# Two weight loads shared between SyncE and GpSimd, and a new order for the opening of an attention-and-experts kernel

## The chip, the cores and the metric

One core of a Trainium2 chip runs the whole program. The metric is device time in microseconds (us): the median of three runs of the kernel before is 735.4 us (737.32, 734.79, 735.40).

## What is computed

Three layers follow one another, all in float32 precision:

```python
f = 1 / (1 + exp(-f_logit))                                # [4, 8, 768, 48]
for t in range(768):                                       # decayed linear attention, per batch and head
    state = f[:, :, t, :, None] * state + einsum('bhd,bhe->bhde', k[:, :, t], v[:, :, t])
    y[:, :, t] = einsum('bhd,bhde->bhe', q[:, :, t], state)
x = y.transpose(0, 2, 1, 3).reshape(3072, 384)
h = x @ w_in                                               # [384, 2048]
x = (h - tanh(h)) @ w_out                                  # [2048, 384]
keep = x @ w_skip > 0                                      # rows that are not kept pass through
e, g = argmax(x @ w_gate), softmax weight of that argmax   # 8 experts, one per row
x[keep] += g * (relu(x @ w1[e]) @ w2[e])                   # [384, 1024], [1024, 384]
```

`w_in` and `w_out` arrive as 8-byte floats. The kernel loads them as pairs of 32-bit words and decodes them on the chip.

## The kernel before

The 3072 rows are cut into 24 units of 128 rows (time chunk c, batch b: unit u = 4c + b). Two units make a block of 256 rows.

**Attention, per unit.** SyncE (SP in the profile) issues the loads of f, k, q and v (`load_f` L288, `load_in` L301), 192 KB each. ScalarE and VectorE form log f. PE multiplies it by a triangle (`pl`, L418). From that come scaled k and q (L433, L436), which PE transposes (`pk`, `pq`, L446). `scores` (L467, L487) multiplies them, VectorE masks the result (L496), and `values` (L508, L515, L521) brings in v. `scores` of a unit waits for `values` of the unit before it, because the two share PSUM buffers. When both units of a block are done, the output is copied out. Small copies inside SBUF, called tails (L549), then move some rows to their place: three of them are issued by GpSimd (POOL) and three by ScalarE in the first blocks. `xhi` and `xlo` (L580, L584) split the block into a high and a low part, `xT`.

**Dense layer.** `gemm1` (L651, "G" below) is nine matmuls for each 128 columns of `w_in`, and `gemm2` (L691, "H") is six for each 128 rows of `w_out`; each float32 product is made of three products of high and low parts. G of block 0 needs `xT` of block 0 and the first decoded columns of `w_in`.

**Weights.** `w_in` comes in four loads w0 to w3 (`load_win`), each of twelve DMAs: six of 192 KB and six small ones of 64 KB, which fill 16 partitions each. `w_out` comes in four loads u0 to u3 (`load_wout`), one DMA of 1536 KB each. Every load goes to one of two staging buffers, so w1 waits until the second half of w0 has been read (step `stt2` of chunk 1). It is decoded in two chunks: ScalarE (`abs`, L190), three VectorE operations (L192, L194, L198), then a split in high and low parts (L368, L372).

**The order.** The first 10 of 12 blocks are written as steps. Each step has an engine, a cost, the steps that it comes after, and a key. `in_order` (L35) simulates them and always takes the step that can begin first; among equals, the one with the smallest key. The order that comes out is the order of instructions on every engine, and each engine then runs its list strictly in that order. Costs and keys are not instructions: they only move other instructions. The lines that set the opening's keys are these:

```python
CHUNK0, CHUNK, LATE = -65, 6, 4
QUEUE = (0, 1, "w", 2, 3, "w", "w", "u", "u", "u", 4, 5, "w", "u")
```

Place i of `QUEUE` gives the key 4i - 200 to f of that unit or to that weight load; k and q of the unit follow with +1 and +2, and v with +8. The loads of units 6 and later wait for the weight load with number `LATE` (4 is w1, 6 is u1). The order on SP before is: f, k, q of unit 0; f, k, q of unit 1; w0; v of units 0 and 1; f, k, q of units 2 and 3; v of 2 and 3; u0; units 4 and 5; w1; u1; units 6 to 9. POOL's list in the opening is `initial` (memsets, ending with L785), the decay of the state of each unit (L569), constants, and the tails.

Of the kernel before, what the change touches and what calls it, by code (L numbers as in the profile page):

```python
# [93 lines left out]
def decay_attention_moe_kernel(  # L94
# [14 lines left out]
    nc = tc.nc  # L109
    P = 128  # L110
    B, H, T, D = q.shape
# [17 lines left out]
    FIRST, NJOIN, NPAY, SKEW = 6, 4, 6, 0  # L129
    EARLIEST, LEAD = -100, 32  # L130
    ALONE = 4
    CHUNK0, CHUNK, LATE = -65, 6, 4
    QUEUE = (0, 1, "w", 2, 3, "w", "w", "u", "u", "u", 4, 5, "w", "u")
    LAG = 2

    cpool = ctx.enter_context(tc.tile_pool(name="cpool", bufs=1, side="left"))
# [49 lines left out]
    def bare(stg, c, mark):  # L186

        u, v = stg[..., 1], stg[..., 0]
        ci = c.bitcast(I32)
        nc.scalar.activation(c, u.bitcast(F32), AF.Abs, scale=2.0**-111, accum_out=mark)  # L190
        yield
        nc.vector.tensor_scalar(ci, ci, 3, None, op0=ALU.logical_shift_left)  # L192
        yield
        nc.vector.scalar_tensor_tensor(  # L194
            out=ci, in0=u, scalar=-0x80000000, in1=ci, op0=ALU.bitwise_and, op1=ALU.bitwise_or
        )
        yield
        nc.vector.scalar_tensor_tensor(  # L198
            out=ci, in0=v, scalar=29, in1=ci, op0=ALU.logical_shift_right, op1=ALU.bitwise_or
        )  # L200
        yield

    def fetch(pool, name, shape, pieces, dst, eng):

        n = pieces[0][3]
        if n == 2 or dst is None:
            t = pool.tile(shape + [2], I32, tag="stg", name=f"stg{name}")
        if n == 2:
            to = t.rearrange("p a w c -> p a (w c)")
        else:  # L210
            to = t = t.bitcast(F32)[..., 0] if dst is None else dst
        for rows, a, src, _ in pieces:
            if len(src.shape) == 3:
                eng.dma_start(to[rows, a], src)
            else:
                for i in range(src.shape[1]):
                    eng.dma_start(to[rows, a.start + i].rearrange("p (w c) -> p w c", w=src.shape[2]), src[:, i])
        return t

    def load(pool, name, shape, pieces, dst):  # L220
# [5 lines left out]
    def words(w):  # L226
        return (w.bitcast(I32), 2) if w.dtype != F32 else (w, 1)
# [48 lines left out]
    more = [rest[:, i * H * 64 : (i + 1) * H * 64].rearrange("p (h d) -> p h d", h=H) for i in range(5)]  # L276
# [6 lines left out]
    NFB = 4  # L283

    def load_f(u):
        c, b = divmod(u, B)
        fx[u] = apool.tile([P, H * D], F32, tag="f", name=f"f{u}", bufs=NFB)
        nc.sync.dma_start(  # L288
            fx[u].rearrange("t (h d) -> t h d", h=H), f_logit[b, :, c * P : (c + 1) * P, :].rearrange("h t d -> t h d")
        )  # L290
# [13 lines left out]
    def exp_f(u):  # L304
        nc.scalar.activation(fx[u], fx[u], AF.Exp, scale=-1.0)
# [10 lines left out]
        nc.scalar.activation(hi, raw, AF.Copy)  # L316
        eng.tensor_tensor(lo, raw, hi.bitcast(F32), ALU.subtract)  # L317

    NWC = 8
    NWL = 4  # L320
    stage = {}

    def load_win(j):

        w = DFF // NWL
        src, m = words(w_in)
        rows = src.rearrange("(h r) (w n c) -> n h r w c", r=D, w=NWL, n=NWL)[j]
        pieces = []
        for jj, (h0, h2, h3) in enumerate(((0, 5, 7), (4, 1, 3))):
            o = 64 * jj  # L330
            pieces.append((slice(o, o + D), slice(0, 2), rows[h0 : h0 + 3 : 2].rearrange("h r w c -> r h w c"), m))
            pieces.append((slice(o, o + D), slice(2, 3), rows[h2 : h2 + 1].rearrange("h r w c -> r h w c"), m))
            pieces.append((slice(o + D, o + 64), slice(0, 3), rows[h3].rearrange("(i r) w c -> r i w c", r=16), m))
        stage["w", j] = fetch(spool, f"w{j}", [P, KT, w], pieces, None, nc.sync)

    def load_wout(j):
# [8 lines left out]
    def unpack(a, j):  # L345

        r = NWC // NWL
        raw = stage[a, j // r]
        if a == "w":
            w = DFF // NWC  # L350
            fs, ss = slice(j * w, (j + 1) * w), slice(j % r * w, (j % r + 1) * w)
            hi, lo = whi[:, :, fs], wlo[:, :, fs]
            raw = raw[:, :, ss]
        else:
            n = NF // NWC
            fs, ss = slice(j * n, (j + 1) * n), slice(j % r * n, (j % r + 1) * n)
            hi, lo = uhi[:, fs], None
            raw = raw[:, ss]
        unit = 1.0
        if (w_in if a == "w" else w_out).dtype != F32:  # L360
            stg, raw = raw, spool.tile([P] + list(hi.shape[1:]), F32, tag="dc", name=f"dc{a}{j}")
            n = 2 * j + (a == "u")
            yield from bare(stg, raw, marks[:, n : n + 1])
            unit = 2.0**-8
        else:
            for _ in range(4):
                yield
        nc.scalar.activation(hi, raw, AF.Copy, scale=unit)  # L368
        yield
        if lo is None:  # L370
            lo = ulo[:, fs]
        nc.vector.scalar_tensor_tensor(  # L372
            out=lo, in0=raw, scalar=unit, in1=hi.bitcast(F32), op0=ALU.mult, op1=ALU.subtract
        )
        yield
# [9 lines left out]
    def step(name, key, eng, cost, emit, *after, take=(), give=(), moved=0.0, lag=0.15):  # L385

        made[name] = x = Step(key, eng, cost, emit, after, take, give, moved, lag)
        steps.append(x)
# [564 lines left out]
    def pieces(gen):  # L953

        return lambda: next(gen, None)

    NCHK = 2 * NWC
    chunks = [(a, j + i) for j in range(0, NWC, 2) for a in "wu" for i in range(2)]

# [13 lines left out]
    line, seen_of = {}, {"w": 0, "u": 0}  # L973
    for i, x in enumerate(QUEUE):
        if x in seen_of:
# [4 lines left out]
    for n, (a, j) in enumerate(chunks):  # L980
        at = CHUNK0 + CHUNK * n
        if n % 2 == 0:
            step(
                ("ld", n), line["wu"[n // 2 % 2], n // 4], "SP", 5.4 if a == "w" else 0.45, (lambda a=a, j=j: (load_win if a == "w" else load_wout)(j // 2)),
                ("stt2", n - 3), moved=5.5 if a == "w" else 4.5,
            )
        more = pieces(unpack(a, j))
        step(("abs", n), at, "ACT", 0.9, more, ("ld", n - n % 2), ("lo", n - 2))
        step(("shift", n), at, "DVE", 0.56, more, ("abs", n))
        step(("stt1", n), at, "DVE", 0.95, more, ("shift", n))  # L990
        step(("stt2", n), at, "DVE", 0.95, more, ("stt1", n))
        step(("hi", n), at, "ACT", 0.84, more, ("stt2", n))
        step(("lo", n), at, "DVE", 0.95, more, ("hi", n), ("ulo", 0) if a == "u" else None)
        made["lo" + a, j] = made["lo", n]


    for u in range(NU):
        blk, half = divmod(u, 2)
        e = EARLIEST + 6 * u if u < FIRST else NF * blk - LEAD + 6 * half - 8

        def get(nm, u=u):
            return lambda: load_in(nm, u)

        if u >= FIRST and (u - FIRST) % NFB == 0:
            us = range(u, min(u + NFB, NU))
            for w in us:
                step(("f", w), e - 20, "SP", 0.45, (lambda w=w: load_f(w)), ("pl", w - NFB), ("ld", LATE), moved=1.2)
            for w in us:
                step(("exp", w), e, "ACT", 0.51, (lambda w=w: exp_f(w)), ("f", w))
                step(("min", w), e, "DVE", 0.36, (lambda w=w: min_f(w)), ("exp", w))  # L1010
            step(("lns", u), e, "ACT", 2.6 + 0.5 * len(us), (lambda us=us: ln_f(us)), *[("min", w) for w in us])
            for w in us:
                made["ln", w] = made["lns", u]
        elif u < FIRST:
            step(("f", u), line[u], "SP", 0.45, (lambda u=u: load_f(u)), ("pl", u - NFB), moved=1.2)
            step(("exp", u), e, "ACT", 0.51, (lambda u=u: exp_f(u)), ("f", u))
            step(("min", u), e, "DVE", 0.36, (lambda u=u: min_f(u)), ("exp", u))
            step(("ln", u), e, "ACT", 0.5, (lambda u=u: ln_f([u])), ("min", u))
        w = -1 if u < 4 else u - 4 if u < 6 else u - 2
        hold = ("ld", LATE) if u >= FIRST else None  # L1020
        step(("k", u), line.get(u, e - 19) + 1, "SP", 0.45, get("k"), ("mk", w), hold, moved=1.2)
        step(("q", u), line.get(u, e - 19) + 2, "SP", 0.45, get("q"), ("mq", w), hold, moved=1.2)
        step(("v", u), line.get(u, e - 18) + 8, "SP", 0.45, get("v"), ("values", w), hold, moved=1.2)
        attend(u)


# [5 lines left out]
    for n, (b, f) in enumerate(slots):  # L1032
# [12 lines left out]
        if n < len(slots) - LAG:  # L1045
            p = homes.get(b, "po")
# [5 lines left out]
            if f == NF - 1:  # L1052
                for u in (2 * b, 2 * b + 1):
# [5 lines left out]
                    r = pieces(route(u))  # L1059
                    at = n + LAG + 2 + 7 * (u % 2 if b > 1 else u)  # L1060
# [167 lines left out]
    for g in range(NF2, E * NF2 + LAG):  # L1228
        e, f = divmod(g, NF2)
# [260 lines left out]
```

## Time and profile before

| what | us |
|---|---|
| median of three runs | 735.4 |
| the profiled execution | 737.04 |
| its span in the trace | 734.9 |
| PE busy in the span | 696.7 (95%) |
| VectorE / ScalarE / POOL busy | 491.9 / 367.0 / 283.2 |

The span is what the trace covers; the 2.1 us between it and the execution's time lie around it. PE is the engine of the matrix products. DVE is VectorE, ACT is ScalarE, SP is SyncE, which only issues DMAs; a letter q behind a name is the engine's DMA or instruction queue.

### The profile page before, as it was taken

Reading aid. Unit: us, or ns where it says so; the run is one execution under the profiler, and the core shown is the slowest. Engines: PE = TensorE matmul, PEld = TensorE weight load, DVE = VectorE, ACT = ScalarE, POOL = GpSimd, SP = SyncE. Lnnn points to the kernel's source line nnn. Section 1 sums busy time; section 2 is a strip of 40 time slices with the busy share of each in tenths; the row PEclk is TensorE's granted clock in tenths of the full one; section 3 lists DMA queues with packets and bytes.
Section 4 is the critical chain, followed back from the end, with each engine's and each line's share of the span. In section 5 each row is a group of like instructions: output and inputs, shape, how many; then the busy total and the mean of one; then the engine's idle time right before and its main releaser. Section 6 shows DMA issues by size and latency. Waiting matters only on the chain. (4 is left out here: it accounts for less than half of the span.)

```text
span 734.9 us, 16491 instructions
## 1 busy us (share of the span) xinstructions
PE 696.7 (95%) x6168; PEld 655.8 (89%) x6168; DVE 491.9 (67%) x1390; ACT 367.0 (50%) x882; POOL 283.2 (39%) x316
## 2 busy tenths in 40 slices
PE   5889989999999999999999999999989899999993
PEld 3678989999998999999999999999989689999993
DVE  2678999678777968768685775845583845655530
ACT  3576786446444465456545444444434435555530
POOL 1232443423344343442434343434543314555641
PEclk9999999999999999999999999999999999999997
DMA  9979793833321312222221220033002667666500
GB/s 155 234 136 220 160 158 80 310 64 72 76 39 40 80 37 70 44 61 44 63 61 28 60 42 32 2 97 115 13 28 71 205 202 236 213 207 211 175 14 22
DMA packets 152688, 76.77 MB, mean 104 GB/s; under 512 B 113864, under 2 KB 149337, under 8 KB 152470
## 3 DMA queue, kind: packets, MB, share of 16 engines
q1 hardware_dynamic: 149462, 70.48, 38.6%
q0 software_dynamic: 2848, 5.00, 1.9%
q8 instruction: 50, 0.82, 0.5%
q14 instruction: 40, 0.33, 0.2%
q10 hardware_dynamic: 288, 0.15, 0.1%
HBM read 61.60 MB, written 15.86 MB: 105 GB/s over the span
## 5 line engine op out<-in xcount | busy, mean ns | idle before, releaser
L674 POOL TENSOR_TENSOR gs<-th,gs 128x256 fp32r<-128x256 f32 x190 | 168.1, 889 | 249.5 <-ACT gs L668 225.0
L691 PE MATMUL po<-uhi,gs 128*128 128x384 f32 x768 | 230.6, 343 | 2.0 <-POOL gs L674 1.8
L651 PE MATMUL ph<-xT,whi 128*128 128x256 f32 x1152 | 219.9, 287 | 2.7 <-DVE th L663 1.8
L651 PEld LDWEIGHTS ph<-xT,whi 128*128 128x128 f32 x1152 | 183.9, 189 | 8.0 <-DVE th L663 3.6
L651 PE MATMUL ph<-xT,wlo 128*128 128x256 f32 x576 | 162.6, 282 | 0.0
L691 PEld LDWEIGHTS po<-uhi,gs 128*128 128x128 f32 x768 | 142.4, 190 | 6.4 <-POOL gs L674 3.8
L663 DVE TENSOR_TENSOR th<-ph,th 128x256 f32<-128x256 f32 x192 | 79.9, 419 | 90.8 <-ACT th L658 90.1
L233 DVE CUSTOM_DVE_ANT_0 scr<-pay,wb 128x384 f32<-128x384 f32 x198 | 128.0, 647 | 7.9 <-ACT pay L699 4.1
L691 PE MATMUL po<-ulo,gs 128*128 128x384 f32 x384 | 129.8, 338 | 0.4 <-DVE ulo L372 0.4
L658 ACT ACTIVATE th<-ph 128x256 f32<-128x256 f32 x192 | 72.7, 381 | 113.2 <-PE ph L651 75.9
L668 ACT ACTIVATE gs<-th 128x256 fp32r<-128x256 f32 x192 | 79.2, 416 | 96.4 <-DVE th L663 92.7
L651 PEld LDWEIGHTS ph<-xT,wlo 128*128 128x128 f32 x576 | 109.5, 190 | 0.0
L691 PEld LDWEIGHTS po<-ulo,gs 128*128 128x128 f32 x384 | 73.2, 191 | 0.7 <-DVE ulo L372 0.7
L1150 PE MATMUL eh<-xt,w 128*128 128x256 f32 x504 | 69.6, 283 | 0.0
L1174 PE MATMUL eo<-w,h 128*128 128x384 f32 x336 | 69.1, 342 | 0.0
L1150 PEld LDWEIGHTS eh<-xt,w 128*128 128x128 f32 x504 | 67.0, 188 | 0.4
L1174 PEld LDWEIGHTS eo<-w,h 128*128 128x128 f32 x336 | 56.3, 188 | 0.0
L1159 DVE SCALAR_TENSOR_TENSOR h<-eh,h 128x256 fp32r<-128x256 f32 x56 | 23.7, 423 | 45.5 <-ACT h L1158 45.5
L1158 ACT ACTIVATE h<-eh 128x256 fp32r<-128x256 f32 x56 | 21.5, 385 | 61.9 <-PE eh L1150 61.8
L732 POOL DMA_INDIRECT xs<-pay,di x24 | 25.7, 1069 | 65.5 <-DVE sm L245 31.2
L317 POOL TENSOR_TENSOR w<-r,w 128x768 fp32r<-128x768 f32 x24 | 44.1, 1846 | 12.3 <-ACT w L316 12.2
L891 POOL DMA_INDIRECT out_dram<-yo,xa x16 | 15.7, 979 | 69.3 <-DVE yo L899 33.6
(189 smaller groups left out, 927.8 us busy)
## 6 DMA issues: line engine op xcount, KB each, us to landing
r<-in_moe_w_dram SPq DMA_DIRECT2D x56, 384.0 KB, 5.1
stgu<-in_moe_w_out_dram SPq DMA_DIRECT2D x4, 1536.0 KB, 7.0
f<-in_f_logit_dram SPq DMA_DIRECT2D x24, 192.0 KB, 3.5
stgw<-in_moe_w_in_dram SPq DMA_DIRECT2D x24, 192.0 KB, 5.5
out_dram<-pay SPq DMA_DIRECT2D x24, 192.0 KB, 2.9
k<-in_k_dram SPq DMA_DIRECT2D x22, 192.0 KB, 3.3
q<-in_q_dram SPq DMA_DIRECT2D x22, 192.0 KB, 3.3
v<-in_v_dram SPq DMA_DIRECT2D x22, 192.0 KB, 2.8
```

The costliest lines, as they stand in the source:

```text
L233: nc.vector.tensor_tensor_reduce(out=scr, in0=x, in1=wb[:, n], scale=1.0, scalar=0.0, op0=ALU.mult, op1=ALU.add, accum_out=lg[:, n : n + 1])
L317: eng.tensor_tensor(lo, raw, hi.bitcast(F32), ALU.subtract)
L651: nc.tensor.matmul(ph, lhsT=w[:, i, fs], rhs=x[:, i, a], start=(n == 0), stop=(n == 3 * KT - 1))
L658: nc.scalar.activation(th, ph, AF.Tanh)
L663: nc.vector.tensor_tensor(th, ph, th, ALU.subtract)
L668: nc.scalar.activation(t[:, 0], th, AF.Copy)
L674: eng.tensor_tensor(t[:, 1], th, t[:, 0].bitcast(F32), ALU.subtract)
L691: nc.tensor.matmul(po[blk, s], lhsT=t[:, a, ss], rhs=w[:, f], start=(f == 0 and n == 0), stop=(f == NF - 1 and n == 2))
L732: nc.gpsimd.indirect_dma_start(xs[:, :], bass.IndirectOffsetOnAxis(ap=di[:, :], axis=0), pt[:, :], None, bounds_check=E * NT - 1, oob_is_e ...
L1150: nc.tensor.matmul(ph, lhsT=a1[:, w, i, f * P : (f + 1) * P], rhs=xt[:, i, a], start=(n == 0), stop=(n == 3 * KT - 1))
L1159: nc.vector.scalar_tensor_tensor(out=h[:, 1], in0=ph, scalar=0.0, in1=h[:, 0].bitcast(F32), op0=ALU.max, op1=ALU.subtract)
L1174: nc.tensor.matmul(eo[e, s], lhsT=h[:, a, ss], rhs=a2[:, w, f], start=(f == 0 and n == 0), stop=(f == NF2 - 1 and n == 2))
```

## The change

The six small DMAs of w0 and of w1 are issued by `nc.gpsimd`, that is by POOL; those of w2 and w3 stay on SP. A step ("by", n) without instructions of its own stands for POOL's time in the plan. The costs of the DMA issues in the plan are other ones, `QUEUE` has another order, v has the key +15 in place of +8, and `CHUNK0` and `LATE` are changed.

```diff
+    VAT = 15
-    CHUNK0, CHUNK, LATE = -65, 6, 4
-    QUEUE = (0, 1, "w", 2, 3, "w", "w", "u", "u", "u", 4, 5, "w", "u")
+    CHUNK0, CHUNK, LATE = -60, 6, 6
+    QUEUE = (0, 1, "w", 2, 3, "w", "w", "u", 4, 5, "w", "u", "u", "u")
...
-        for rows, a, src, _ in pieces:
+        for rows, a, src, _, *other in pieces:
+            by = other[0] if other else eng
             if len(src.shape) == 3:
-                eng.dma_start(to[rows, a], src)
+                by.dma_start(to[rows, a], src)
...
-    NWC = 8
+    NWC, NPOOL = 8, 2
...
-            pieces.append((slice(o + D, o + 64), slice(0, 3), rows[h3].rearrange("(i r) w c -> r i w c", r=16), m))
+            pieces.append((slice(o + D, o + 64), slice(0, 3), rows[h3].rearrange("(i r) w c -> r i w c", r=16), m, nc.gpsimd if j < NPOOL else nc.sync))
...
-                ("ld", n), ..., "SP", 5.4 if a == "w" else 0.45, ...
+                ("ld", n), ..., "SP", (3.9 if j // 2 < NPOOL else 7.6) if a == "w" else 0.7, ...
+        if a == "w" and j % 2 == 0 and j // 2 < NPOOL:
+            step(("by", n), line["w", n // 4], "POOL", 5.0, lambda: None, ("stt2", n - 3), ("init", 0), lag=2.0)
-        step(("abs", n), at, "ACT", 0.9, more, ("ld", n - n % 2), ("lo", n - 2))
+        step(("abs", n), at, "ACT", 1.1, more, ("ld", n - n % 2), ("by", n - n % 2) if j // 2 < NPOOL and a == "w" else None, ("lo", n - 2))
...
-            step(("f", u), line[u], "SP", 0.45, ...
+            step(("f", u), line[u], "SP", 0.8, ...
-        step(("v", u), line.get(u, e - 18) + 8, "SP", 0.45, get("v"), ("values", w), hold, moved=1.2)
+        step(("v", u), line.get(u, e - 18) + VAT, "SP", 0.8, get("v"), ("values", w), hold, moved=1.2)
```

The steps of k and q change their cost from 0.45 to 0.8 in the same way.

## Rows read from the trace of the kernel before

**Rows 1.** Page: PE's busy time (share, instructions); DMA's busy tenths in 40 slices

```profile
PE 696.7 (95%) x6168; PEld 655.8 (89%) x6168; DVE 491.9 (67%) x1390; ACT 367.0 (50%) x882; POOL 283.2 (39%) x316
DMA  9979793833321312222221220033002667666500
```

**Rows 2.** Windows by stage, PE alone: stretch, PE busy, clock, DMA share, GB/s

```profile
10.00:15.00 5.00, 4.32 (x36) 1.00 1.16 145
15.00:20.00 5.00, 2.29 (x9) 1.00 1.30 153
...
62.00:91.00 29.00, 28.92 (x307) 1.00 0.85 178
```

**Rows 3.** PE's waits, 0 to 110 us: total us, times, longest

```profile
PE pl L421 <- DVE lfs L409: 1.7, 1, 1.7
...
PE pq L446 <- ACT uhi L368: 1.4, 1, 1.4
...
PE ph L651 <- DVE xT L584: 0.6, 1, 0.6
PE po L691 <- DVE ulo L372: 0.4, 1, 0.4
PE ph L651 <- ACT xT L580: 0.3, 1, 0.3
```

**Rows 4.** SP's timeline: start, us, issue, count

```profile
5.31 8.37 SPq L217 DMA_DIRECT2D stgw<-in_moe_w_in_dram  x12
13.72 1.21 SPq L301 DMA_DIRECT2D v<-in_v_dram  x2
15.24 3.44 SPq L288 DMA_DIRECT2D f<-in_f_logit_dram  x1
...
21.50 0.85 SPq L301 DMA_DIRECT2D early<-in_k_dram  x1
22.39 2.28 SPq L301 DMA_DIRECT2D early<-in_q_dram  x1
...
41.16 13.93 SPq L217 DMA_DIRECT2D stgw<-in_moe_w_in_dram  x12
```

**Rows 5.** SP's timeline, 6.0 to 6.7 us and 12 to 13.7 us alone

```profile
5.31 1.42 SPq L217 DMA_DIRECT2D stgw<-in_moe_w_in_dram  x2
...
12.47 1.21 SPq L217 DMA_DIRECT2D stgw<-in_moe_w_in_dram  x2
```

**Rows 6.** PE's timeline: start, us, operation, count, [idle before <- releaser]

```profile
20.21 1.95 PE L508 MATMUL py<-A,v 128*48 128x128 f32 x16 [1.65 <-DMA v<-in_v_dram]
...
31.06 0.59 PE L521 MATMUL pu<-ident,en 128*64 128x1 f32 x16
31.59 0.65 PE L446 MATMUL pk<-ident,early 128*112 128x128 f32 x4
...
34.20 0.55 PE L467 MATMUL ps<-qT,kT 48*64 48x128 f32 x8 [0.88 <-ACT qT L453]
```

**Rows 7.** Windows of the lull, all engines: PE, PEld, DVE, ACT, POOL busy, clock, DMA

```profile
56.00:58.00 2.00, 1.49 (x10) 1.20 (x11) 2.00 (x4) 2.00 (x5) 0.00 (x0) 0.95 0.66 127
58.00:60.00 2.00, 2.00 (x13) 1.56 (x17) 1.81 (x3) 1.62 (x4) 0.00 (x0) 0.50 1.00 389
60.00:62.00 2.00, 2.00 (x49) 1.83 (x42) 0.30 (x2) 0.00 (x0) 0.00 (x0) 0.70 1.06 366
```

**Rows 8.** POOL's timeline

```profile
24.39 0.68 POOL L569 TENSOR_TENSOR S<-S,dd 112x192 f32<-112x192 f32 x1 [20.23 <-DVE S L559]
...
33.39 1.74 POOL L549 DMA_DIRECT2D early<-early  x3
41.26 0.68 POOL L569 TENSOR_TENSOR S<-S,dd 112x192 f32<-112x192 f32 x1 [6.13 <-DVE S L559]
...
52.10 1.50 POOL L549 DMA_DIRECT2D xf<-tm  x3
```

**Rows 9.** Page, costliest groups: the dearest DMA issue on POOL

```profile
L732 POOL DMA_INDIRECT xs<-pay,di x24 | 25.7, 1069 | 65.5 <-DVE sm L245 31.2
```

More of the change, by code (lines that the diff above doesn't have):

```diff
@@ L211, in fetch @@
             to = t = t.bitcast(F32)[..., 0] if dst is None else dst
-        for rows, a, src, _ in pieces:
+        for rows, a, src, _, *other in pieces:
+            by = other[0] if other else eng
             if len(src.shape) == 3:
-                eng.dma_start(to[rows, a], src)
+                by.dma_start(to[rows, a], src)
             else:
                 for i in range(src.shape[1]):
-                    eng.dma_start(to[rows, a.start + i].rearrange("p (w c) -> p w c", w=src.shape[2]), src[:, i])
+                    by.dma_start(to[rows, a.start + i].rearrange("p (w c) -> p w c", w=src.shape[2]), src[:, i])
         return t
@@ L983, in decay_attention_moe_kernel @@
             step(
-                ("ld", n), line["wu"[n // 2 % 2], n // 4], "SP", 5.4 if a == "w" else 0.45, (lambda a=a, j=j: (load_win if a == "w" else load_wout)(j // 2)),
+                ("ld", n), line["wu"[n // 2 % 2], n // 4], "SP", (3.9 if j // 2 < NPOOL else 7.6) if a == "w" else 0.7, (lambda a=a, j=j: (load_win if a == "w" else load_wout)(j // 2)),
                 ("stt2", n - 3), moved=5.5 if a == "w" else 4.5,
             )
+        if a == "w" and j % 2 == 0 and j // 2 < NPOOL:
+            step(("by", n), line["w", n // 4], "POOL", 5.0, lambda: None, ("stt2", n - 3), ("init", 0), lag=2.0)
         more = pieces(unpack(a, j))
-        step(("abs", n), at, "ACT", 0.9, more, ("ld", n - n % 2), ("lo", n - 2))
+        step(("abs", n), at, "ACT", 1.1, more, ("ld", n - n % 2), ("by", n - n % 2) if j // 2 < NPOOL and a == "w" else None, ("lo", n - 2))
         step(("shift", n), at, "DVE", 0.56, more, ("abs", n))
@@ L1014, in decay_attention_moe_kernel @@
         elif u < FIRST:
-            step(("f", u), line[u], "SP", 0.45, (lambda u=u: load_f(u)), ("pl", u - NFB), moved=1.2)
+            step(("f", u), line[u], "SP", 0.8, (lambda u=u: load_f(u)), ("pl", u - NFB), moved=1.2)
             step(("exp", u), e, "ACT", 0.51, (lambda u=u: exp_f(u)), ("f", u))
@@ L1020, in decay_attention_moe_kernel @@
         hold = ("ld", LATE) if u >= FIRST else None
-        step(("k", u), line.get(u, e - 19) + 1, "SP", 0.45, get("k"), ("mk", w), hold, moved=1.2)
-        step(("q", u), line.get(u, e - 19) + 2, "SP", 0.45, get("q"), ("mq", w), hold, moved=1.2)
-        step(("v", u), line.get(u, e - 18) + 8, "SP", 0.45, get("v"), ("values", w), hold, moved=1.2)
+        step(("k", u), line.get(u, e - 19) + 1, "SP", 0.8, get("k"), ("mk", w), hold, moved=1.2)
+        step(("q", u), line.get(u, e - 19) + 2, "SP", 0.8, get("q"), ("mq", w), hold, moved=1.2)
+        step(("v", u), line.get(u, e - 18) + VAT, "SP", 0.8, get("v"), ("values", w), hold, moved=1.2)
         attend(u)
```

## The prediction

> **What bounds the kernel now.** I read the page first: PE is busy for 696.7 of 734.9 us, and the slices show the DMA engines near full in the first tenth of the span and idle in most of the rest [rows 1]. So the kernel is bound by PE as soon as PE has work, and what an edit of the opening can win is PE's idle or slowed time there. I then read PE alone by stage. From 62 to 91 us it is busy for 28.92 of 29 us: no order can win there. In 15 to 20 us it is busy for 2.29 of 5, while DMA stands at a share of 1.30 and moves only 153 GB/s; a share over 1 means that packets queue at the engines [rows 2]. The third view is PE's waits up to 110 us: 0.6 and 0.3 us at the first G, 1.4 and 0.4 us in a lull near 56 us, and 1.7 us for log f of units 6 and later at 91 us [rows 3]; before them its timeline has 1.65 us for v of unit 0 [rows 6]. Last, the windows of the lull: behind it PE's granted clock falls to 0.50, its lower level of 1.2 GHz, in 58 to 60 us, and is a mean of 0.70 in the next two and 0.95 in the two before [rows 7]. That costs 2 x 0.5 + 2 x 0.3 + 2 x 0.05 = 1.7 us of full-speed work.
>
> **The change, part by part.**
>
> *The six small issues of w0 leave SP.* Two small issues take 1.21 us, two large ones 1.42, and all twelve 8.37 [rows 4, 5]. SP's share becomes 6 x 0.71 = 4.3 us, so SP ends w0 at 9.6 us and not at 13.7. POOL waits 20.23 us before its work at 24.39, thus from 4.2 us on [rows 8], and issues its six there. The trace shows no such issue on POOL. From below, a 16 KB tail takes 1.50 / 3 = 0.5 us [rows 8]; from above, an indirect one takes 1.07 us [rows 9]. That is 3.0 to 6.4 us, all in POOL's gap: no cost. Bytes stay the same.
>
> *v moves behind f, k, q of unit 2.* By key, SP's list is now w0, f2, k2, q2, v0, f3, k3, q3, v1. Three loads at 0.85 us put v0's issue near 12.2 us, 1.5 us before the 13.72 of the trace [rows 4]. But 3 x 192 KB (0.59 MB) more stand in front of it, and at the 153 GB/s of that stretch [rows 2] they take 3.9 us. If SP bound, v0 would come 1.5 us earlier; if the DMA engines do, up to 3.9 us later. The share of 1.30 and SP's issue of f2, which was held for 3.44 us [rows 4], speak for the engines. I take 3.9 - 1.5 = +2.4 us, for `values` of unit 0 at 20.21 us [rows 6] and for all that hangs on it.
>
> The Trainium skill, on the page "DMA: Bandwidth & Descriptors", section "Issuing engines are not separate DMA queues", says that issues from several engines end on the same 16 engines and save only the sequencer's time. By that rule moving the six brings nothing here, since the queue behind SP is full; this is the second rival below. The share over 1 agrees.
>
> *Unit 2 is ready early.* Before, its transposes began at 31.59 us, after `values` of unit 1 had ended at 31.06 + 0.59 = 31.65, and its scores followed at 34.20, with a wait of 0.88 us in between [rows 6]: 2.55 us on the path. A q of that stretch was issued with a stall until 24.67 us [rows 4]; now that of unit 2 is issued near 12 us, and the transposes fit into waits for the mask of unit 1. Two groups of 0.65 us and the wait make 2.2 us; the rest of the 2.55 is log f of unit 3 on PE, which stays. I take -2.0 us (bounds 0 and -2.55).
>
> *First G.* Its two waits, 0.3 and 0.6 us [rows 3], come from the tails of block 0. With unit 3 loaded sooner, the scores of unit 3 can fill them: -0.9 us (bounds 0 and -0.9).
>
> *The lull at 54 to 62 us.* PE waits 1.4 + 0.4 + 0.3 us there; the 0.3 is a wait for a scaled k, too short to have a row here. G of block 1 waits for `xT` of block 1, that is for unit 3, which is ready earlier by what is won above. DVE and ACT, however, are busy for all of 56 to 58 us [rows 7], so the lull is partly theirs and need not go. I take half, -1.0 us (bounds 0 and -2.1), and half of the clock's loss, -0.8 us (bounds 0 and -1.7).
>
> *w1.* SP gave it from 41.16 to 55.09 us, twelve issues for 13.93 us against 8.37 for w0 [rows 4], so it will be in its buffer several us sooner. This hides fully: what needs it lies in the stretch where PE is busy for 28.92 of 29 us [rows 2]. On POOL its six issues wait for the staging buffer, and whatever stands behind them in POOL's list waits too. In the gap between the tails of block 0 (ended by 35.1 us) and the decay at 41.26 us [rows 8] they cost nothing, 3.0 to 6.4 us in a gap of 6.13. I take 0; the bad place is the third rival.
>
> *The rest.* The hold of units 6 and later on u1 changes nothing, as they already stood behind u1. `CHUNK0`, v of later units and the plan's costs only reorder work beneath a full PE: 0, with bounds of 1.7 us on either side for the wait at 91 us, which a new order can lose or double [rows 3].
>
> *The sum:* +2.4 - 2.0 - 0.9 - 1.0 - 0.8 = -2.3 us. The profiled execution took 737.04 us, a span of 734.9 and 2.1 around it, so it would take 734.7. It stands 1.6 us above the median of the runs; against the median the forecast is 735.4 - 2.3 = 733.1 us.
>
> **The rivals.**
>
> *Larger gain.* The small pieces land by a queue of their own and v0 is bound by SP: -1.5 us instead of +2.4. The lull and its clock dip then go wholly: -1.5 - 2.55 - 0.9 - 2.1 - 1.7 = -8.8 us at most. For it: every term has its row. Against it: full DMA engines, and full DVE and ACT in the lull. I expect -4.5 to -8.8: 726.6 to 730.9 us, 728.5 as its middle.
>
> *No change.* The DMA engines set the opening. v0 comes +3.9 us later, unit 2 gives back 2.0 and the first G 0.9, and the lull stays as it is: +1.0, thus 736.4 us, with 734.3 to 737.4 around it. For it speak the shares of 1.16 and 1.30 from 10 to 20 us [rows 2].
>
> *Slower: POOL's tails behind w1.* If POOL's list has the six pieces of w1 before the tails of block 0 (33.39 us [rows 8]), and the buffer comes free only shortly before, the tails start 3.0 to 6.4 us late, and `xT` of block 0 and the first G with them. PE can cover about 2.1 us with the scores of unit 3, so 0.9 to 4.3 us remain. With +2.4 for v0 and -2.0 for unit 2, and nothing won in the lull, that is +1.3 to +4.7 us: 736.7 to 740.1, with 738.4 as its middle. It decides from the moment at which the output of unit 1 is ready before POOL has issued the last piece. For it: w1 is now planned earlier, and the buffer was freed only near 33 us before. Against it: the plan counts 5 us of POOL for it and knows the tails.
>
> The Trainium skill, "SBUF — State Buffer", section "A bandwidth-pool intuition that's wrong (but worth ruling out)", gives a DMA issued by GpSimd 620 ns alone and about 3100 ns beside a VectorE copy that holds the shared port. By its figure the six would take 18.6 us, an estimate, and this rival would cost over 10 us. The tails on POOL in this trace took 0.50 to 0.58 us each beside a busy VectorE [rows 8], so I give that size little weight.
>
> **How the numbers follow.** The forecast (-0.5 to -4.5 us, 730.9 to 734.9) has 0.40, the larger gain 0.17, no change 0.18, slower 0.25. What a measurement can tell from no change is 0.3%, or 2.2 us. Of the forecast's 0.40, 0.25 lies beyond -2.2 us, so faster is 0.25 + 0.17 = 0.42. Of the slower rival's 0.25, 0.03 lies within 2.2 us, so slower is 0.22, and the same is 0.15 + 0.18 + 0.03 = 0.36. The range runs from 728.8 to 738.4: it leaves out the lower half of the larger gain (0.08) and the upper half of the slower rival (0.12).
>
> **What would show it.** Right: in the new trace the wait for v of unit 0 still exists, with v landing at 21 to 24 us; scores of unit 2 follow `values` of unit 1 without transposes in between; the first G waits under 0.3 us; the granted clock after 54 us stays near 1. Wrong: the first G later than 42 us behind POOL's pieces of w1; the DMA share well below 1 before 25 us; a new wait of PE over 2 us anywhere in 62 to 110 us, which would make the prediction fail whatever the opening wins.

## The result, and the profile after

The changed kernel takes 744.03 us (median of 4 runs, 742.4 to 745.15) against 736.36 us for the kernel before (4 runs on the same chip, 734.79 to 738.49): a ratio of 1.0105, with an interval of 1.0077 to 1.0134. It is slower by 7.7 us. The forecast was 733.1 us, and the time lies outside its range of 728.8 to 738.4. The profiled execution took 743.65 us (span 741.7).

The page shows PE with nearly the same busy time as before, 694.6 against 696.7 us [rows 1], in a span that is 6.8 us longer. The extra time is therefore idle time of PE, not more work.

```profile
PE 694.6 (94%) x6168; PEld 656.4 (89%) x6168; DVE 489.7 (66%) x1390; ACT 367.3 (50%) x882; POOL 294.4 (40%) x328
```

PE's waits of the first 115 us (total, times, longest) begin with one that the kernel before does not have [rows 3]:

```profile
PE pg L808 <- DMA wg<-in_moe_w_skip_dram: 6.6, 1, 6.6
PE pl L420 <- ACT f L314: 5.1, 1, 5.1
PE py L510 <- DMA v<-in_v_dram: 3.8, 1, 3.8
```

`pg` is the turn of the router's gate weights: three transposes of `wg`, which stand in this order just ahead of the first G. PE's timeline of after (start, us, operation, count, [idle before <- releaser]), which answers to [rows 6]:

```profile
22.34 1.95 PE L510 MATMUL py<-A,v 128*48 128x128 f32 x16 [3.84 <-DMA v<-in_v_dram]
...
34.91 0.60 PE L523 MATMUL pu<-ident,en 128*64 128x1 f32 x16
35.44 0.65 PE L448 MATMUL pk<-ident,early 128*112 128x128 f32 x4
35.92 0.60 PE L448 MATMUL pq<-ident,early 128*112 128x128 f32 x4
36.45 0.45 PE L469 MATMUL ps<-qT,kT 48*64 48x128 f32 x8
...
47.18 0.60 PE L523 MATMUL pu<-ident,en 128*64 128x1 f32 x16
54.37 0.80 PE L808 MATMUL pg<-ident,wg 128*9 128x128 f32 x3 [6.60 <-DMA wg<-in_moe_w_skip_dram]
54.83 0.78 PE L653 MATMUL ph<-xT,whi 128*128 128x256 f32 x2
```

From 47.78 to 54.37 us PE does nothing, and the first G, ready behind it in PE's list, starts at 54.83. Why `wg` was late stands in SP's timeline of after (start, us, issue, count), beside which [rows 4] can be laid:

```profile
5.50 4.30 SPq L219 DMA_DIRECT2D stgw<-in_moe_w_in_dram  x6
...
12.33 6.02 SPq L303 DMA_DIRECT2D early<-in_q_dram  x1
18.40 0.77 SPq L303 DMA_DIRECT2D v<-in_v_dram  x1
...
41.59 3.81 SPq L219 DMA_DIRECT2D stgw<-in_moe_w_in_dram  x6
45.50 0.71 SPq L303 DMA_DIRECT2D v<-in_v_dram  x1
46.25 0.58 SPq L801 DMA_DIRECT2D wg<-in_moe_w_gate_dram  x1
46.88 2.14 SPq L802 DMA_DIRECT2D wg<-in_moe_w_skip_dram  x1
...
144.45 5.56 SPq L706 DMA_DIRECT2D out_dram<-pay  x4
```

and in the same view of the kernel before, in lines not shown earlier:

```profile
39.10 0.65 SPq L799 DMA_DIRECT2D wg<-in_moe_w_gate_dram  x1
39.80 0.48 SPq L800 DMA_DIRECT2D wg<-in_moe_w_skip_dram  x1
...
137.32 5.38 SPq L704 DMA_DIRECT2D out_dram<-pay  x4
```

Before, SP issued both gate-weight loads ahead of w1. After, they stand behind w1's six pieces and one more v: issued at 46.25 and 46.88 instead of 39.10 and 39.80 us. The first store of a finished block moves from 137.32 to 144.45 us, 7.1 us later, and that offset stays to the end. So the loss is complete before 137 us.

The wait also costs clock. The windows of after, PE alone (stretch, its length, PE busy and instructions, granted clock, DMA share, GB/s), answer to [rows 2, 7]:

```profile
10.00:15.00 5.00, 4.37 (x36) 1.00 1.14 172
15.00:20.00 5.00, 2.24 (x9) 1.00 1.29 160
...
52.00:54.00 2.00, 0.00 (x0) 0.50 0.08 7
54.00:56.00 2.00, 1.63 (x8) 0.50 0.00 0
56.00:58.00 2.00, 2.00 (x14) 0.67 0.51 62
```

PE comes back from the wait at 0.50 (its 1.2 GHz level) and is at a mean of 0.67 in the next two us. That is 1.63 x 0.50 + 2.00 x 0.33 = 1.5 us more. With the 6.6 the account is 8.1 us for a loss of 7.7; the rest of the change would be worth about -0.4 us. That rest includes the lull of the kernel before: its clock dip is as large (a mean of 0.79 from 54 to 62 us in both traces), and in after this dip stands in its place. The row of 52 to 54 us shows something else: the DMA engines are nearly idle (0.08, 7 GB/s) while PE still waits for a transfer.

How could a change of other issues move the gate weights? `constants` runs as POOL's step `("const", 0)`, planned after the mask of unit 1. That mask follows the scores of unit 1, these follow `values` of unit 0, and these wait for v of unit 0. `VAT` puts v later in the plan: v of unit 0 lands at 22.6 us of the plan's own time in place of 19.0, and `constants` begins at 31.3 in place of 25.3. At the same time VectorE's unpacking of w0 comes earlier in the plan, so the step that loads w1 begins at 25.6 in place of 29.4. The two cross, and `constants` is emitted behind w1. Its two loads go to SP's real list, though the plan counts no time of SP for them: it neither sees them there nor keeps them ahead of w1. When the plan is worked out with one of the changed numbers set back at a time, only `VAT` back to 8 puts `wg` ahead of w1 again; in the kernel before, 15 in place of 8 is enough to push it behind. The costs and `QUEUE` alone do neither.

### The profile page after: what moved, and what is told of

Same layout as the page of the kernel before. It is cut to its first block, busy times and chain, and to the rows that moved or that the text cites. A ratio compares the mean times of both kernels' runs of the same rounds, so it can differ in the third digit from the quotient of the medians.

```text
span 741.7 us, 16516 instructions
## 1 busy us (share of the span) xinstructions
PE 694.6 (94%) x6168; PEld 656.4 (89%) x6168; DVE 489.7 (66%) x1390; ACT 367.3 (50%) x882; POOL 294.4 (40%) x328
## 5 line engine op out<-in xcount | busy, mean ns | idle before, releaser
L676 POOL TENSOR_TENSOR gs<-th,gs 128x256 fp32r<-128x256 f32 x190 | 170.0, 898 | 241.1 <-ACT gs L670 216.9
```

The costliest lines, as they stand in the source:

```text
L676: eng.tensor_tensor(t[:, 1], th, t[:, 0].bitcast(F32), ALU.subtract)
```

## The experiments

Theory A: the slowdown is the gate weights' place in SP's list, and the rest of the change is worth about nothing. Rival B: later v, POOL's issues or the new order cost it, and the wait for `wg` only stands where another would. Ratios are against runs of the kernel before that were taken beside those of the experiment; its medians there were 737.44, 737.82 and 737.32 us.

**Gate weights early, in the changed kernel.** The two loads are issued right behind `dec`; nothing else changes.

```diff
     def preset():
         nc.sync.dma_start(dec, turned.pop()[:NU].rearrange("u p a -> u (p a)"))
+        nc.sync.dma_start(wg[:, :, :E], w_gate.rearrange("(k p) e -> p k e", p=P))
+        nc.sync.dma_start(wg[:, :, E], w_skip.rearrange("(k p) -> p k", p=P))
 ...
     def constants():
 ...
-        nc.sync.dma_start(wg[:, :, :E], w_gate.rearrange("(k p) e -> p k e", p=P))
-        nc.sync.dma_start(wg[:, :, E], w_skip.rearrange("(k p) -> p k", p=P))
```

> The changed kernel with one difference: the two small DMAs of the gate weights (wg, 12 KB and 1.5 KB) are issued on SP right behind the decay rows (dec), ahead of the v load of unit 4 and of w1, and not behind w1 and both v loads. The plan and the list of every other engine stay as in the changed kernel. Theory A (the whole loss is PE standing in its list at the gate's transpose until w_skip lands): the wait of 6.6 us goes, and with it about 1.4 us of PE at its lower clock behind it, so the time falls by 8 us from 744.0 to about 736, and the ratio to the kernel before is 0.995 to 1.003. Rival B (the loss is the later v of unit 0, the fuller DMA queue and POOL's issues; the gate's wait only shows lateness that would appear elsewhere): another wait of several us takes its place near 48 to 55 us, and the time stays above 741, ratio over 1.006.

Measured: 737.68 us, ratio 0.9999 (0.9974 to 1.0023). PE's timeline, and under it SP's, show the wait gone:

```profile
22.48 1.95 PE L510 MATMUL py<-A,v 128*48 128x128 f32 x16 [3.95 <-DMA v<-in_v_dram]
...
47.80 0.50 PE L808 MATMUL pg<-ident,wg 128*9 128x128 f32 x3
48.05 0.48 PE L653 MATMUL ph<-xT,whi 128*128 128x256 f32 x2
```

```profile
41.29 0.39 SPq L792 DMA_DIRECT2D wg<-in_moe_w_gate_dram  x1
41.73 0.47 SPq L793 DMA_DIRECT2D wg<-in_moe_w_skip_dram  x1
...
137.07 5.37 SPq L706 DMA_DIRECT2D out_dram<-pay  x4
```

The first store comes 7.4 us earlier than in after. Moving two small loads by 5 us takes back the whole loss, and what is left of the change measures as nothing, within 0.3% either way.

**The turn late, in the changed kernel.** The loads stay late, but PE meets the turn only after the eighth G.

```diff
-    step(("turn", 0), ..., ("const", 0), ("scores", 2), ("preset", 0), take=(("pa", "gate"),), lag=0.25)
+    step(("turn", 0), ..., ("const", 0), ("scores", 2), ("preset", 0), ("G", 7), take=(("pa", "gate"),), lag=0.25)
```

> The changed kernel with one difference: the transpose of the gate weights on PE is made to come after the eighth G in the plan, so that it stands later in PE's list; its DMAs stay where the change put them, behind w1. Theory A: PE no longer meets the gate weights before they have landed, so the wait goes as in the run with early DMAs: 735 to 738 us, ratio 0.998 to 1.004; the plan behind 50 us differs a little, which is worth 1 us either way. Rival B: above 741 us, ratio over 1.006, with a wait for another operand between 48 and 56 us.

Measured: 739.02 us, 1.0007 (0.9984 to 1.003). `pg` runs at 72.33 us without a wait, and the first store is at 138.47. The loads may be late, then; what cost the time was PE's fixed place for their use. This cures it from the other side.

**Gate weights late, in the kernel before.** The reverse: only the two loads move, behind w1.

```diff
         stage["w", j] = fetch(spool, f"w{j}", [P, KT, w], pieces, None, nc.sync)
+        if j == 1:
+            nc.sync.dma_start(wg[:, :, :E], w_gate.rearrange("(k p) e -> p k e", p=P))
+            nc.sync.dma_start(wg[:, :, E], w_skip.rearrange("(k p) -> p k", p=P))
```

> The kernel before with one difference: the two DMAs of the gate weights are issued behind w1 (SP's twelve issues, which ended at 55.1 us) and not ahead of the v load of unit 5. Plan and lists of the other engines are those of the kernel before, where PE reaches the gate's transpose at 45 us. Theory A: PE stands there until the weights land, at about 57 to 61 us, that is 12 to 16 us less what the lull at 54 to 62 us (2.1 us of waits and 1.7 us of clock) already cost: 745 to 751 us, ratio 1.011 to 1.020. Rival B (that place in SP's list matters little): 736 to 739 us, ratio under 1.004.

Measured: 747.96 us, 1.0122 (1.009 to 1.0153). SP's timeline and PE's:

```profile
40.43 10.33 SPq L217 DMA_DIRECT2D stgw<-in_moe_w_in_dram  x12
50.81 0.58 SPq L336 DMA_DIRECT2D wg<-in_moe_w_gate_dram  x1
51.44 0.49 SPq L337 DMA_DIRECT2D wg<-in_moe_w_skip_dram  x1
```

```profile
55.93 0.80 PE L807 MATMUL pg<-ident,wg 128*9 128x128 f32 x3 [10.03 <-DMA wg<-in_moe_w_skip_dram]
```

The kernel before, with no other edit, loses as the changed one does. Together the three experiments show the place of `wg` against its use to be enough for a loss of this size, and needed for it in this plan.

**The six issues on POOL, in the kernel before.** Only the emission; the plan does not change.

```diff
-            pieces.append((slice(o + D, o + 64), slice(0, 3), rows[h3]..., m))
+            pieces.append((slice(o + D, o + 64), slice(0, 3), rows[h3]..., m, nc.gpsimd if j < 2 else nc.sync))
```

> The kernel before with one part of the change alone: the six small DMAs of w0 and of w1 are issued by POOL; plan, costs, keys and all lists otherwise as before. Theory A (POOL's issues are harmless, and the loss lies in the new order): 733 to 737 us, ratio 0.995 to 1.002; w0 leaves SP 4 us earlier, the queue behind stays full, and w1 is issued in 4 to 6 us and not in 13.9. Rival C (DMAs issued by POOL are themselves dear, by slow landing or by holding POOL's list before the tails): 739 us or more, ratio over 1.004.

Measured: 739.98 us, 1.0027 (1.0003 to 1.0051): between what the two theories gave, and inconclusive. It brings no gain in this order, and if it costs anything, it is about 2 us. POOL's twelve issues took 3.28 and 3.06 us in this run. SP came to v of units 0 and 1 earlier, at 10.22 us instead of 13.72 [rows 4], but was held there, and PE waits 2.6 us for v of unit 0 instead of 1.65 [rows 6]:

```profile
10.22 3.98 SPq L302 DMA_DIRECT2D v<-in_v_dram  x2
```

So SP's time was not what v waited for. Where the 2 us went was not isolated. The profiled execution is one of the longest of this kernel's twelve (742.28 us, of 735.75 to 742.69), and it lost most by its clock, in a stretch where the kernel before has 1.00:

```profile
40.00:54.00 14.00, 12.60 (x131) 0.63 1.05 149
```

**The six issues on SP, in the kernel with the gate weights early.** Against the first experiment.

```diff
-            ... m, nc.gpsimd if j < NPOOL else nc.sync))
+            ... m, nc.sync))
```

> The changed kernel with the gate's DMAs early, and the small pieces of w0 and w1 issued by SP again, in an otherwise unchanged plan: what is left of the change is its order alone. If POOL's issues bring nothing because the DMA engines are full anyway (the rival 'no change' of the prediction), this is as fast as the run with early gate DMAs and POOL's pieces (737.7 us): ratio to the kernel before 0.998 to 1.003. If the 4 us of SP's time that POOL takes over do reach the path, v of unit 0 lands up to 4 us later than there (PE waits up to 8 us for it, against 3.9) and the ratio is 1.004 to 1.008.

Measured: 740.84 us, 1.0037 (1.0014 to 1.0061), between the two forecasts, and 4.48 us of wait for v against 3.95. That is about 0.4% more than in the first experiment, but the two intervals overlap, so what POOL's help is worth in the new order stays open. The wait for v makes only 0.5 us of the 3. In the profiled execution more of it is clock; this run, and under it the first experiment:

```profile
40.00:54.00 14.00, 12.33 (x145) 0.70 0.60 101
40.00:54.00 14.00, 11.76 (x207) 1.00 0.91 145
```

That is 12.33 x 0.30 = 3.7 us of full-speed work. Why the clock falls in the one order and not in the other was not isolated.

**v of unit 0 early again (`VAT` 8 and 3), gate weights early.**

```diff
-    VAT = 15
+    VAT = 8     # and in a second kernel: 3
```

> The changed kernel with the gate's DMAs early and the key of v at +8 as before, so that v of units 0 and 1 stand right behind w0 again. If the later v is what eats the gain of the new order, PE's wait for v of unit 0 falls from 3.9 to 0.5 to 1.7 us, and the time by 2 to 3 us: ratio 0.995 to 0.998. If the bytes only change places, so that unit 2 is late instead, the ratio stays within 0.998 to 1.003.

> The changed kernel with the gate's DMAs early and the key of v at +3: v of units 0 and 1 stand ahead of w0, right behind their own f, k and q. If PE's early path, in which values of unit 0 waits for v until 22.5 us, is what the opening can still win, PE has no wait for v of unit 0, values of unit 0 begin near 16 us, and although w0 lands 2 to 3 us later the time falls by 2 to 5 us: ratio 0.993 to 0.997. If w0 is what binds, PE meets a wait of the same size at the first G and the ratio is 0.998 to 1.003.

Measured: 744.5 us, 1.0096 (1.0065 to 1.0127) for 8, and 744.64 us, 1.0097 (1.0068 to 1.0126) for 3. Both miss both forecasts: the wait for v falls to 1.2 us, or goes, and the kernel is slower by 7 us. PE's waits from 58 to 165 us, with `VAT` 8:

```profile
PE ph L653 <- DVE th L665: 4.2, 5, 1.2
PE po L693 <- DVE ulo L374: 1.6, 2, 1.3
PE pk L448 <- DVE kp L435: 1.3, 2, 1.1
PE po L693 <- POOL gs L676: 1.3, 2, 0.7
```

With 15 the first line is 1.4 us and the others are absent. The wait for v is not what this order should be judged by: when v comes early, the plan lays the chunks' unpacking and the units differently, and PE has waits for DVE that the order with 15 does not have. First stores at 146.95 and 145.01 us, against 137.07, agree with a loss that is complete by then. Which step of the plan does it was not isolated.

**v of unit 0 earlier, in the kernel before** (the key's `+ 8` to `+ 3`).

```diff
-        step(("v", u), line.get(u, e - 18) + 8, "SP", 0.45, ...
+        step(("v", u), line.get(u, e - 18) + 3, "SP", 0.45, ...
```

> The kernel before with one number changed: v's key is +3 and not +8, so that v of units 0 and 1 stand ahead of w0; all issues on SP, old costs and old queue. If the place of v is the lever and neither POOL nor the measured costs are, this gains as much as the changed kernel with early gate DMAs and the same key: ratio 0.993 to 0.997. If the rest of the change matters, it stays within 0.998 to 1.003 while that one gains.

Measured: 737.39 us, 1.0 (0.9983 to 1.0017). Neither theory holds as it was put, since the changed kernel with the same key did not gain. The wait is no lever here either; the opening lost as much elsewhere, with a granted clock of 0.50 from 25 to 40 us in the profiled execution.

**v of unit 0 later, in the kernel before** (`+ 15`), alone, and then with the gate weights early as in the first experiment.

```diff
-        step(("v", u), line.get(u, e - 18) + 8, "SP", 0.45, ...
+        step(("v", u), line.get(u, e - 18) + 15, "SP", 0.45, ...
```

> The kernel before with one number of the change: v's key is +15 in place of +8. The lists then have the gate's two DMAs behind all twelve issues of w1. If this number alone, by way of that place, is the cause, PE shows a wait of 5 to 15 us at the gate's transpose and the time is 743 to 752 us, ratio 1.008 to 1.020. If POOL's part or the new queue is needed for the loss, there is no such wait and the ratio is under 1.005.

> The same, with the gate's two DMAs issued right behind the decay rows, all else as in the run with +15 alone. If the later v costs only through the gate, the ratio is 0.998 to 1.005 and no wait at the gate's transpose is left. If the later v costs by itself (v of unit 0 lands later, as the prediction priced at +2.4 us), it stays at 1.005 or more with a wait of over 4 us for v of unit 0.

Measured: alone 752.81 us, 1.0203 (1.0158 to 1.0248); with the gate weights early 741.25 us, 1.0058 (1.0034 to 1.0082). SP and PE with `+ 15` alone:

```profile
42.51 8.96 SPq L217 DMA_DIRECT2D stgw<-in_moe_w_in_dram  x12
51.51 0.58 SPq L799 DMA_DIRECT2D wg<-in_moe_w_gate_dram  x1
52.14 0.49 SPq L800 DMA_DIRECT2D wg<-in_moe_w_skip_dram  x1
```

```profile
23.60 1.65 PE L418 MATMUL pl<-f,tri 128*128 128x384 f32 x2 [5.00 <-ACT f L312]
...
57.46 0.80 PE L806 MATMUL pg<-ident,wg 128*9 128x128 f32 x3 [8.87 <-DMA wg<-in_moe_w_skip_dram]
```

So the key of v, one number, does push the gate weights behind w1 by itself, and the time came out just above the range expected. Of its 2.0%, about 1.45% is that (11.6 us between the two kernels, of which the wait is 8.87). The remaining 0.6% comes with the later v alone, but its interval reaches across the 1.005 that was to decide, and the wait for v that was expected is not there: in both kernels PE waits 5 us for log f in its place. With the gate weights early PE is also busy for only 23.67 us from 62 to 91 us, against 28.92 before [rows 2]; which of the two makes the 0.6% was not isolated. The first store comes at 143.68 us there, 6.4 us later than before, though the profiled execution is only 2.4 us longer (739.39 against 737.04): in this order the first store does not tell what is lost in the end.

## Why the prediction was wrong

**The bound** was read rightly: PE, and its idle time in the opening. What decided the result is idle time of PE in the opening, only new.

**The step that failed is "The rest".** It said that `CHUNK0`, v of later units and the plan's costs "only reorder work beneath a full PE: 0, with bounds of 1.7 us on either side". It priced the later v of units 0 and 1 by v's arrival and never followed the steps that hang on v in the plan. One of them, `constants`, is POOL's in the plan but issues on SP, so its place in SP's list is set by whatever is emitted ahead of it. With `wg` behind w1, and its transposes at a fixed place in PE's list, this came to 6.6 us of wait and 1.5 of clock; that this place is the cause is shown by the first three experiments. The stretch was not beneath a full PE either: the statement rests on 62 to 91 us [rows 2], and the wait is at 48 to 54.

**v of unit 0** (+2.4): right. `values` of unit 0 start at 22.34 instead of 20.21 us, +2.1. SP's issue of q of unit 2 was held for 6.02 us (3.44 for that of f, at about the same time, before [rows 4]), and DMA stands at 1.14 and 1.29. With POOL's issues alone SP came to v 3.5 us earlier and PE waited longer for it. So the engines bound it, not SP.

**Unit 2 early** (-2.0): wrong, about 0. Scores of unit 2 come at 36.45 instead of 34.20, +2.25: all of v's delay was kept. The term put its transposes into "waits for the mask of unit 1", and the kernel before has no such waits; its window from 25 to 31 us is full:

```profile
25.00:31.00 6.00, 6.00 (x61) 1.00 0.95 227
```

The transposes did go ahead, and log f of unit 3 with them, but there they lengthen the way: `values` of unit 1 end 13.17 us after the start of those of unit 0 (22.34 to 34.91 + 0.60), in place of 11.44 (20.21 to 31.65 [rows 6]). That eats the 1.6 us by which the step from there to the scores became shorter, 0.94 instead of 2.55; and in that step the transposes of unit 3 (35.44 and 35.92 us) took the place of those of unit 2.

**First G** (-0.9) and **the lull** (-1.8 with its clock): the kernel with the gate weights early shows these freed of `wg`. The first G has no wait, as forecast, since the scores of unit 3 now run ahead of it; but it starts at 48.05 us, long after the place of its old waits (39.84 us on PE's timeline before), so the work was exchanged more than the waits were filled. Its windows, PE alone:

```profile
54.00:62.00 8.00, 6.98 (x80) 1.00 0.82 246
62.00:91.00 29.00, 27.31 (x266) 1.00 0.73 168
91.00:100.00 9.00, 8.85 (x50) 0.81 1.04 147
```

and of the kernel before:

```profile
54.00:62.00 8.00, 6.13 (x67) 0.79 0.75 241
...
91.00:100.00 9.00, 7.13 (x49) 1.00 0.72 108
```

The lull's dip of the clock is gone, 0.79 to 1.00 over 8 us; but one of the same size stands behind the wait for log f, 0.81 over 9 us, where the kernel before has the wait and no dip. That wait of 1.7 us [rows 3] only falls earlier, to 89 to 91 us instead of 91 to 93, so most of what 62 to 91 us lost is this wait moved into it. The net of all terms, with `wg` out of the way, is the ratio of 0.9999 (0.9974 to 1.0023): nothing, within 2 us, against the predicted -2.3 us. The first stores agree (137.07 against 137.32 us).

**w1 and POOL's issues** (0): right. SP's share of w0 took 4.30 us, as forecast. POOL's six took 3.29 us and 3.03 us, 0.55 and 0.51 each, near the lower bound, and ended long before the tails of block 0. POOL's timeline of after, which answers to [rows 8]:

```profile
4.11 3.29 POOL L219 DMA_DIRECT2D stgw<-in_moe_w_in_dram  x6
26.68 3.03 POOL L219 DMA_DIRECT2D stgw<-in_moe_w_in_dram  x6 [19.29 <-DVE S L561]
...
35.69 1.53 POOL L551 DMA_DIRECT2D early<-early  x3 [4.65 <-ACT early L543]
```

**The rivals.** The slower rival had the right side, but the wrong place and too small a size (736.7 to 740.1 us): POOL's tails did not stand behind w1. The Trainium skill, "SBUF — State Buffer", section "A bandwidth-pool intuition that's wrong (but worth ruling out)", has about 3100 ns for a DMA issued by GpSimd that overlaps with a VectorE copy. No run here tests that figure: an issue took 0.55 us at most, but VectorE was busy for only 0.45 of the 3.29 us and 1.06 of the 3.03 us of these issues. Nor was it busy throughout beside the tails that the prediction set against the figure (0.57 of 1.74 us and 0.94 of 1.50 us). "No change" is what the change is worth without the gate weights. The Trainium skill, "DMA: Bandwidth & Descriptors", section "Issuing engines are not separate DMA queues", says that issues from several engines run on the same 16 engines and save only the sequencer's time; the old order agrees, where moving the six brought no gain (1.0027), and the new one leaves it open. Two signs that were named for a failure came in part. A new wait of PE over 2 us came, but at 48 to 54 us, outside the stretch that was watched. The first G was later than 42 us (54.83, and 48.05 with the gate weights early), but not behind POOL's pieces.

## What to carry to other kernels

When an order is planned with costs and due times, look for DMAs that a step issues on another engine's queue than the one it is planned on: they have no place of their own in the plan of that queue and land wherever the emission puts them. Before pricing a reorder, follow each moved step to every step that hangs on it, and for each small load ask which big burst it may fall behind and which in-order engine meets its use at a fixed place. Shortening one wait of an opening says little by itself: three kernels here removed or shortened a wait for v and none was faster.

## What the runs showed of the hardware that was not expected

- The load of `w_skip`, 384 pieces of 4 bytes, let PE go 5.3 us after its issue ended in after (49.02 to 54.37), 4.0 in the kernel before with the gate weights late (51.93 to 55.93) and 4.8 with v later (52.63 to 57.46). In all three it stands behind pieces of w1, although in after the DMA engines were almost idle at the end of that time. In the kernel before with v earlier it stands ahead of w1, and there it let PE go 1.9 us after its issue ended (42.04 to 43.95). A load of 1.5 KB is not quick because it is small: its place counts.
- An issue on POOL of a 64 KB piece took 0.51 to 0.55 us, as long as one of a 16 KB tail [rows 8] and a little less than the 0.60 that SP took for one of the same pieces in a full queue (1.21 / 2 [rows 5]).
- One kernel, run again, can differ in time with its granted clock. With the six issues on SP and the gate weights early, twelve runs go from 736.85 us at a mean clock of 0.993 to 743.32 us at 0.979, nearly as much as the whole loss of this change. It is not so in every kernel: in the kernel before with v earlier, 736.33 us and 739.48 us have nearly the same clock (0.982 and 0.983).
- After the wait of 6.6 us the granted clock was 0.50 for the first 1.6 us of PE's work and 0.67 in the next two us. A wait of 1.7 us for log f is followed by a dip (0.81 over 9 us) in the kernel with the gate weights early and by none (1.00) in the kernel before, so the length of one wait did not tell whether the clock falls.
